# A Fourier-mixing and attention kernel: the sequence DFT as seven products of quarter blocks, and four of five chunks of the output projection moved into the loop

## The chip, the core and the metric

The kernel runs on one core of a Trainium2 chip. A core has a matrix engine (TensorE, PE in the profile; its weight loads are shown apart as PEld), a vector engine (VectorE, DVE), an engine for activation functions (ScalarE, ACT), a general engine (GpSimd, POOL) and one that issues the kernel's DMAs (SyncE, SP; its queue is SPq). They run side by side and wait for each other on semaphores. Data lies in DRAM, in SBUF (128 partitions) and in PSUM, the eight banks that matmuls write. The metric is the device time of one execution in microseconds (us); less is better.

## What is computed

Inputs are x (2048 x 640), the DFT matrices of the sequence (2048 x 2048, real and imaginary) and of the hidden dimension (640 x 640, real and imaginary), the weights of an attention with 32 query heads of width 20 and one shared key/value head, and a gate vector. All is float32.

```python
# A: Fourier mixing                       # B: attention, S=2048, D=640, H=32, Dh=20
a = x @ dft_hid_re.T                      q = (x @ wq) split into 32 heads
b = x @ dft_hid_im.T                      k, v = x @ wk, x @ wv          # shared by all heads
A = dft_seq_re @ a - dft_seq_im @ b       o = softmax(q k^T / sqrt(20)) v
                                          B = concat(o) @ wo
g = sigmoid(sum(x * gate_w, -1))
out = g * A + (1 - g) * B
```

## The kernel before

Float32 products are made from three matmuls: each operand is split into a high part (rounded) and a low part (the rest), and high x high, high x low and low x high are summed in PSUM. The split of one operand is a cast and a subtraction.

A **place** is one pair of matmuls of 64 rows by 320 columns on the two halves of the array (`halves.put` queues a pair, `halves.run` emits one of its two matmuls, written y0 and y1 below). All of part A is done in places: first 64 groups of 15 places make a and b (tile names `ab`, 960 places), then 64 groups of 48 places make the sequence DFT (tile name `y`, 3072 places). A group fills two PSUM banks (F0, F1); when its last matmul is done ACT copies both banks to SBUF (`y_evict`, entries E0 and E1), POOL adds the two halves, and the next group may use the banks.

The rest of the kernel is the attention. `a_unit` makes scores for the row maximum (PE matmul `a`, DVE `mx`), `b_unit` makes them again transposed and takes the exponential (PE `b`, ACT `pt`), `av_step` multiplies by v (PE `av`, V in the plans). The order on PE is written out by hand: 256 rounds `(p, qh, kk)`, head pair by half of the queries by pair of key blocks, each following a list (`AB15`, `Y16`, `Y12`, `N12`) that says in which order the a, b, y, E and V entries go. There are 48 rounds of AB15 with 15 places, 144 of Y16 with 16 places, 54 of Y12 and 10 of N12 with 12 places; N12 has no `a` left to do. A round ends with E0 E1 V V, and the V of a round belongs to the b of the round before. The entries of a round call the generator `f_stream` for as many places as the round has, and with them the loads and splits that the generator issues between its places.

In the DFT stage before, one block of 128 rows by 1024 of the DFT matrix is loaded (`load_c`, 512 KB), split by POOL (`split_c`: `ch` L465, `cl` L466) and used twice, for the two halves of the columns (48 places); the transformed x, split, lies in SBUF (`ab`).

After the last round, the output projection stands alone: `o_group` is called 32 times (16 token blocks, 2 column halves) and makes 5 chunks x 3 = 15 matmuls of 128 rows by 320 columns each, then DVE scales and adds part A (`oy` L558), and SP writes 128 x 320 numbers of the output. The attention output `oT_d` and the broadcast reciprocal of the softmax sums `rx_d` come through DRAM (`load_o`, `mult_o`, `split_o`). `finish_half` ends a half of a head pair: ACT copies the sums and outputs out of PSUM (`ob`), SP writes them to `sum_d` and `oT_d` and reads the sums back reshaped (`sm`); `finish_sums` or, for the last head pair, `finish_last` takes the reciprocal on DVE (`rc`), writes it (`rec_d`) and broadcasts it to 20 rows (`rx_d`). The last half of the last pair is finished after the first `o_group`, and its data are needed by the 17th.

The order on PE, ACT, DVE and POOL is the order in the code. The order on SP is chosen by the scheduler when the program is built and is then fixed, so a DMA that waits holds back the DMAs behind it. `later(n, f, ...)` calls f after n ticks, and a round has four ticks.

Of the kernel before, what the change touches and what calls it, by code (L numbers as in the profile page):

```python
# [17 lines left out]
P = 128  # L18
# [15 lines left out]
def kernel(  # L34
# [30 lines left out]
    class Rot:  # L65
# [11 lines left out]
    ab_d = {  # L77
        (j, e): dram.tile([P, 4 * HALF], F32, name=f"ab_d{j}{e}") for j in range(SJ) for e in range(2)
# [6 lines left out]
    y0_d = dram.tile([S, D], F32, name="y0_d")  # L85
# [204 lines left out]
    PHASES = ((1, 0), (0, 0), (1, 1), (0, 1))  # L290
    XSEQ = [SJ * half + j for half, e in PHASES for j in range(SJ)]
# [165 lines left out]
    def load_c(sh, tb, i):  # L457
        raw = raw_tile([P, SJ, P], "craw")
        move(raw, (cre, cim)[i][tb, sh])
        return raw  # L460

    def split_c(raw):
        n = free_c.pop(0)
        h, l = [c_slot(2 * n + z, [P, SJ, P], F32R, "ch cl".split()[z]) for z in range(2)]
        nc.gpsimd.tensor_copy(h, raw)  # L465
        nc.gpsimd.tensor_tensor(l, raw, h.bitcast(F32), op=ALU.subtract)  # L466
        return h, l, n

    first_c = {}
# [4 lines left out]
    yp = []  # L474

    TW = 2 * P
    wos, oraw, ospl, yrow = {}, {}, {}, {}

    def spare(k, name):
        if k % 4 < 2:  # L480
            return yp[0].tile([P, D], F32, tag=f"spare{k % 4}", name=name, bufs=1)
        return cpool.tile([P, D], F32, tag=f"raw{k % 4 - 2}", name=name)

    wo_raw = {}

    def load_wo(c):
        wo_raw[c] = spare(c % 2, "woraw")
        move(wo_raw[c], wo[c * P : (c + 1) * P])

    def split_wo(c):  # L490
        raw = wo_raw.pop(c)
        if c < 3:
            if c == 0:
                wos["at"] = [t[:, : 3 * HALF] for t in qbuf[:3]]
                wos["at"].append(c_slot(2 * free_c[0], [P, 3 * HALF], F32R, "wo"))
            at = [wos["at"][k // 3][:, k % 3 * HALF : (k % 3 + 1) * HALF] for k in range(4 * c, 4 * c + 4)]
        else:
            t = abp.tile([P, 4, HALF], F32R, tag=f"ab{c - 3}0", name=f"wo{c}")
            at = [t[:, k] for k in range(4)]
        for e in range(2):  # L500
            h, l, r = at[2 * e], at[2 * e + 1], raw[:, e * HALF : (e + 1) * HALF]
            nc.vector.tensor_copy(h, r)
            nc.vector.tensor_tensor(l, r, h.bitcast(F32), op=ALU.subtract)
            wos[c, e] = (h, l)

    oT_v = oT_d.rearrange("(c p) t -> p c t", p=P)
    rx_v = rx_d.rearrange("(c p) t -> p c t", p=P)
    NO = S // TW

    def load_o(n):  # L510

        if n < NO:
            oraw[n] = []
            for k, v in enumerate((oT_v, rx_v)):
                if (n % 2, k) == (1, 1):
                    t = yp[0].tile([P, KC, TW], F32, name="oraw", bufs=1)
                else:
                    t = abp.tile([P, KC, TW], F32, tag=f"ab{5 + 2 * (n % 2) + k}0", name="oraw")
                move(t, v[:, :, n * TW : (n + 1) * TW])
                oraw[n].append(t)  # L520

    def mult_o(n):
        if n < NO:
# [25 lines left out]
    def o_group(tb, e):  # L549
        n, k = divmod(tb, 2)  # L550
        es, tk = slice(e * HALF, (e + 1) * HALF), slice(k * P, (k + 1) * P)
        rows = slice(tb * P, (tb + 1) * P)
        ps = orot(f"o_{tb}_{e}")[:, :HALF]
        h, l = ospl[n]
        for c in range(KC):
            mm3(ps, h[:, c, tk], l[:, c, tk], *wos[c, e], KC, c)
        oy = yp[0].tile([P, HALF], F32, tag=("yt", "yu")[e], name="oy")
        nc.vector.scalar_tensor_tensor(  # L558
            oy, ps, omg[:, tb : tb + 1], yrow[tb][:, es], op0=ALU.mult, op1=ALU.add
        )  # L560
        move(out[rows, es], oy)
# [33 lines left out]
    def ab_sum(grp):  # L595
# [5 lines left out]
        if stage["loop"]:  # L601
            ab_low()
# [102 lines left out]
    def f_stream():  # L705
# [293 lines left out]
```

## Time and profile before

| | |
|---|---|
| median of 3 runs | 1797.76 us (1797.14 to 1797.78) |
| profiled execution, its own time | 1797.24 us |
| its span, first to last instruction | 1795.5 us |
| PE busy | 1782.3 us, 99% of the span |
| DVE, ACT, POOL busy | 1390.7, 1231.5, 551.9 us |
| DMA traffic | 156.44 MB, mean 87 GB/s |

The profile is of one execution. Its own time is 1.74 us more than its span, and 0.52 us less than the median. "Busy" of PE is modelled, since matmuls overlap: the durations of single matmuls are longer than the distance at which they start. Idle time of an engine that nothing waits for costs nothing.

### The profile page before, as it was taken

What the parts mean: (1) busy time and instruction counts of PE and PEld (TensorE: products, weight loads), DVE (VectorE), ACT (ScalarE), POOL (GpSimd) and SP (SyncE); (2) the same over time, 40 slices, a digit from 0 to 9 for tenths busy, and PEclk for the clock granted to TensorE, in tenths of its full rate; (3) what the DMA queues carried; (4) which work ended last, traced back from release to release, by engine and by line L of the source; (5) the groups of instructions that cost most, each with busy time, mean ns of one, the idle gap of its engine ahead of it and who ended that gap; (6) DMA issues with size and microseconds to landing.
All of it is one profiled execution on the core that took longest, in us unless ns stands there. A gap on an engine that the chain in (4) does not pass through costs nothing.

```text
span 1795.5 us, 42902 instructions
## 1 busy us (share of the span) xinstructions
PE 1782.3 (99%) x17112; PEld 1286.0 (72%) x17112; DVE 1390.7 (77%) x2319; ACT 1231.5 (69%) x2421; POOL 551.9 (31%) x492
## 2 busy tenths in 40 slices
PE   8999999999999999999999999999999999999999
PEld 6797677767777777777777777777776666666689
DVE  4498888888888888888888888888888888888334
ACT  3347878887777767777767777776777777777830
POOL 3056575555222221212212123222321221122131
PEclk9999999999999999999999999999999999999999
DMA  7652123211211221111121552222121211111376
GB/s 245 196 184 93 50 87 113 91 51 51 89 48 47 66 64 56 52 56 59 50 65 40 175 178 72 68 63 63 57 66 51 60 48 59 56 52 33 93 226 213
DMA packets 105956, 156.44 MB, mean 87 GB/s; under 512 B 25108, under 2 KB 74772, under 8 KB 105156
## 3 DMA queue, kind: packets, MB, share of 16 engines
q1 hardware_dynamic: 105756, 153.70, 27.2%
q8 instruction: 134, 2.20, 0.5%
q14 instruction: 66, 0.54, 0.1%
HBM read 109.16 MB, written 48.76 MB: 88 GB/s over the span
## 4 chain that ended last, share of the span: by engine, by line
PE 97%; DMA 1%; SPq 1%; DVE 1%; issue 0%; ACT 0%; DVEq 0%; ACTq 0%
PE av L781 26%; PE y L576 23%; PE b L769 19%; PE a L226 15%; PE ab L576 7%; PE o L114 1%; PE o L115 1%; PE o L116 1%; PE q L114 1%; PE q L116 1%; PE q L115 1%; SPq L106 1%; DMA ql_d<-ql 0%; DMA xr<-in_xT_dram 0%; DMA wraw<-in_wq_dram 0%; DVE xl L110 0%
## 5 line engine op out<-in xcount | busy, mean ns | idle before, releaser
L233 DVE TENSOR_REDUCE mx<-a 128x1 f32<-128x512 f32 x2048 | 1278.4, 684 | 269.6 <-PE a L226 228.4
L777 ACT ACTIVATE pt<-b 128x512 f32<-128x512 f32 x2048 | 1074.9, 604 | 365.6 <-PE a L226 284.7
L769 PE MATMUL b<-qs,ks 62*128 62x512 f32 x2048 | 772.8, 415 | 1.7 <-DVE mx L233 1.3
L226 PE MATMUL a<-ks,qs 60*128 60x512 f32 x2048 | 721.1, 410 | 0.2
L576 PE MATMUL y<-ab,ch 64*128 64x320 f32 x4096 | 718.8, 306 | 0.0
L576 PEld LDWEIGHTS y<-ab,ch 64*128 64x128 f32 x4096 | 550.0, 185 | 10.1
L769 PEld LDWEIGHTS b<-qs,ks 62*128 62x128 f32 x2048 | 350.5, 185 | 224.7 <-DVE mx L233 169.4
L576 PE MATMUL y<-ab,cl 64*128 64x320 f32 x2048 | 509.1, 306 | 0.0
L781 PE MATMUL av<-pt,vsb 128*32 128x512 f32 x4096 | 492.5, 598 | 0.0
L226 PEld LDWEIGHTS a<-ks,qs 60*128 60x128 f32 x2048 | 351.4, 185 | 9.9 <-ACT pt L777 1.2
L576 PEld LDWEIGHTS y<-ab,cl 64*128 64x128 f32 x2048 | 320.1, 185 | 6.6
L586 POOL TENSOR_TENSOR yt<-yt,yu 128x320 f32<-128x320 f32 x64 | 55.4, 866 | 696.5 <-ACT yu L581 696.5
L781 PEld LDWEIGHTS av<-pt,vsb 128*32 128x32 f32 x4096 | 106.8, 109 | 223.7 <-issue 214.8
L466 POOL TENSOR_TENSOR cl<-craw,ch 128x1024 fp32r<-128x1024 f32 x64 | 152.8, 2387 | 5.1
L465 POOL CAST ch<-craw 128x1024 fp32r<-128x1024 f32 x64 | 66.6, 1041 | 266.0 <-PE y L576 257.4
L598 POOL TENSOR_TENSOR abt<-abt,abu 128x320 f32<-128x320 f32 x64 | 55.8, 872 | 140.1 <-ACT abu L631 140.1
L576 PE MATMUL ab<-wbh,xh 64*128 64x320 f32 x256 | 58.6, 306 | 0.0
L576 PE MATMUL ab<-wbh,xl 64*128 64x320 f32 x256 | 58.4, 305 | 0.0
L614 POOL TENSOR_TENSOR ab<-abt,ab 128x320 fp32r<-128x320 f32 x64 | 56.2, 878 | 3.9
L576 PE MATMUL ab<-w1l,xh 64*128 64x320 f32 x192 | 50.5, 307 | 0.0
L576 PE MATMUL ab<-w0l,xh 64*128 64x320 f32 x192 | 49.9, 306 | 0.0
L576 PE MATMUL ab<-w0h,xh 64*128 64x320 f32 x192 | 48.3, 308 | 0.0
(103 smaller groups left out, 1427.2 us busy)
## 6 DMA issues: line engine op xcount, KB each, us to landing
craw<-in_cre_dram SPq DMA_DIRECT2D x32, 512.0 KB
craw<-in_cim_dram SPq DMA_DIRECT2D x32, 512.0 KB
xraw<-in_xT_dram SPq DMA_DIRECT2D x32, 320.0 KB
qs<-qh_d SPq DMA_DIRECT2D x128, 80.0 KB
ab_d<-ab SPq DMA_DIRECT2D x16, 640.0 KB
y_d<-yt SPq DMA_DIRECT2D x64, 160.0 KB
ab<-ab_d SPq DMA_DIRECT2D x16, 640.0 KB
xr<-in_xT_dram SPq DMA_DIRECT2D x20, 256.0 KB
```

The source lines that it names most:

```text
L114: nc.tensor.matmul(ps, wh, xh, start=(i == 0), stop=False)
L226: nc.tensor.matmul(ps, qs[v][b : b + 60, qb * P : (qb + 1) * P], ks[b : b + 60, c * ROW : (c + 1) * ROW], start=True, stop=True,)
L233: nc.vector.tensor_reduce(mx[v][:, hh, qb, c : c + 1], ps, axis=AX.X, op=ALU.max)
L465: nc.gpsimd.tensor_copy(h, raw)
L466: nc.gpsimd.tensor_tensor(l, raw, h.bitcast(F32), op=ALU.subtract)
L576: nc.tensor.matmul(ps, w, x, start=start, stop=stop)
L586: nc.gpsimd.tensor_tensor(yt, yt, yu, op=ALU.add)
L598: nc.gpsimd.tensor_tensor(t0, t0, t1, op=ALU.add)
L614: nc.gpsimd.tensor_tensor(lo, t0, hi.bitcast(F32), op=ALU.subtract)
L769: nc.tensor.matmul(ps, ks[b : b + 62, kc * P : (kc + 1) * P], qs[2 * p + qc // 2][b : b + 62, (qc % 2) * ROW : (qc % 2 + 1) * ROW], start= ...
L777: nc.scalar.activation(t, ps, AF.Exp, scale=SCALE)
L781: nc.tensor.matmul(ps[32 * g : 32 * g + 32, :], vsb[:, kc, :], t, start=first, stop=last)
```

## The change

The DFT matrix and the transformed x are cut into quarter blocks, and the 2 x 2 block product is done with seven block products (Strassen's scheme in Winograd's form) where eight were done before. In the code the four A blocks are the upper and the lower 1024 rows of the real and of the imaginary matrix (`a_src`), each 2048 wide. One product has 16 loaded blocks of 128 x 1024 and 8 groups of 48 places, so the seven have 2688 places. The 384 places that are left of 3072 take chunks 0 to 3 of the output projection (32 groups `oo` of 12 places), in the last 32 rounds. The plans of the rounds and their order are as before.

- Every block of a product is loaded, combined from two blocks where the scheme wants a sum (`PRODUCTS`: 64 of 112 blocks, one more POOL operation and one more load each), split, and used once. Two sums are stored to DRAM (`s_d`) and read again.
- The transformed x goes to DRAM unsplit (`b_d`); POOL makes four differences of its blocks during the first product (`sum_t`, to `t_d`), and the operand of products 3 to 7 is loaded and split one product ahead (`load_b`, `split_b`).
- What a product adds to the result is combined on POOL (`y_out`), with partial results that go through DRAM (`part_d`). The gate is applied later, in `o_out`.
- The weights `wo` and the attention output are split on POOL inside the loop, and `o_out` adds the gated part A to the scaled chunks 0 to 3 and leaves the sum in SBUF (`acc`).
- After the loop, `o_group` makes 3 matmuls for chunk 4 instead of 15 for all five, and DVE adds to `acc`. The last 16 of the 32 groups wait for the last half of the last head pair; its reciprocal is now broadcast straight to SBUF (`load_rec`), and product and split are four pieces on DVE (`split_last`).
- `finish_sums` comes 12 ticks after `finish_half` instead of 24, and `finish_half` issues its four sums before its four outputs.

```diff
+    PRODUCTS = (
+        ("p1", (a_src(0, 0),), None, None, None),
+        ("p2", (a_src(1, 0),), None, None, None),
+        ("p5", (a_src(0, 1), a_src(1, 1)), ALU.add, 1, t_d[1]),
+        ("p6", (s_src(1), a_src(0, 0)), ALU.subtract, 2, t_d[2]),
+        ("p7", (a_src(0, 0), a_src(0, 1)), ALU.subtract, None, t_d[3]),
+        ("p3", (a_src(1, 0), s_src(2)), ALU.subtract, None, b_d[1, 1]),
+        ("p4", (a_src(1, 1),), None, None, t_d[4]),
+    )
+    def split_c(g):
+        if g < NP:
+            n, k = divmod(g, NT)
+            raw = c_raw.pop(g)
+            _, _, how, save, _ = PRODUCTS[n]
+            if how:
+                nc.gpsimd.tensor_tensor(raw[0], raw[0], raw[1], op=how)
+            if save:
+                later(3, move, s_d[save][k // 2, k % 2].rearrange("p (j t) -> p j t", j=SJ), raw[0])
...
+            nc.gpsimd.tensor_copy(h, raw[0])
+            nc.gpsimd.tensor_tensor(l, raw[0], h.bitcast(F32), op=ALU.subtract)
...
+    def y_out(name, r, m, parts):
...
+        t = parts[0]
+        add(t, m, ALU.subtract if name == "p4" else ALU.add)
+        if name == "p6":
+            add(parts[1], t)
+            keep("u2", t)
+            keep("u4", parts[1])
+        elif name == "p7":
+            add(parts[1], t)
+            keep("u3", t)
+            done(1, 1, parts[1])
...
+    def o_out(tb, e, m, y0):
...
+        nc.gpsimd.tensor_scalar(y0, y0, gate[:, tb : tb + 1], None, op0=ALU.mult)
+        nc.gpsimd.tensor_tensor(acc[tb][:, e], m, y0, op=ALU.add)
...
+    def load_rec(qh):
+        ts = slice(qh * QT, (qh + 1) * QT)
+        for hh in range(2):
+            b = P - (2 - hh) * DH
+            move(last_o[qh][1][b : b + DH], rec_d[2 * LAST + hh : 2 * LAST + hh + 1, ts].to_broadcast([DH, QT]))
+
+    def split_last(qh, k, n):
...
+        nc.vector.tensor_tensor(o[:, cs], o[:, cs], r[:, cs], op=ALU.mult)
+        nc.vector.tensor_copy(h[:, cs], o[:, cs])
+        nc.vector.tensor_tensor(l[:, cs], o[:, cs], h[:, cs].bitcast(F32), op=ALU.subtract)
...
     def o_group(tb, e):
...
-        for c in range(KC):
-            mm3(ps, h[:, c, tk], l[:, c, tk], *wos[c, e], KC, c)
...
+        mm3(ps, h[:, tk], l[:, tk], *wos[OC, e], 1, 0)
+        t = acc[tb][:, e]
+        nc.vector.scalar_tensor_tensor(t, ps, omg[:, tb : tb + 1], t, op0=ALU.mult, op1=ALU.add)
...
+        for g in range(NP):
...
+            sum_t(g - 1)
+            split_c(g + 1)
+            load_c(g + 2)
+            split_b(g + NT)
+            load_b(g + NT + 1)
...
+        for tb in range(NT):
+            for e in range(2):
+                if e == 0:
+                    split_o(tb + 1)
+                else:
+                    load_o(tb + 2)
...
-            later(24, chores.append, (finish_sums, p, sm))
+            later(12, chores.append, (finish_sums, p, sm))
...
-    for i in range(2 * NT):
+    for i in range(NT):
         tb, e = divmod(i, 2)
         o_group(tb, e)
-        tick()
-        if i == 0:
+        if i == 1:
             for st in old:
                 av_step(*st)
             finish_half(*old[-1][:2])
...
+            load_last(1)
+        elif i >= NT - 4:
+            tick()
+    load_rec(1)
+    for i in range(NT):
+        tb, e = divmod(i, 2)
+        if i % 4 == 0:
+            split_last(1, i // 4, 4)
+        o_group(SJ + tb, e)
```

The first place that the change rewrites is POOL's work between two groups of the DFT. Before, in the second half of the stage, one group of 48 places has this on POOL: `yt` and `yu` are the two halves, `y0` the partial result read back, and the block of the DFT matrix is split once.

```order
L466 TENSOR_TENSOR cl_19242<-craw_19142,ch_19241 128x1024
L586 TENSOR_TENSOR yt_19415<-yt_19415,yu_19416 128x320
L590 TENSOR_TENSOR yt_19415<-yt_19415,y0_19140 128x320
L465 CAST ch_19557<-craw_19447 128x1024
L466 TENSOR_TENSOR cl_19558<-craw_19447,ch_19557 128x1024
```

In the changed kernel one group of the product p6 has this on POOL (`craw` is combined in place, `tb` is the operand of the next product, `part` holds partial results):

```order
L722 TENSOR_TENSOR yt_18051<-yt_18051,yu_18052 128x320
L557 TENSOR_TENSOR part_17747<-part_17747,yt_18051 128x320
L557 TENSOR_TENSOR part_17749<-part_17749,part_17747 128x320
L498 TENSOR_TENSOR craw_17866<-craw_17866,craw_17868 128x1024
L503 CAST ch_18081<-craw_17866 128x1024
L504 TENSOR_TENSOR cl_18082<-craw_17866,ch_18081 128x1024
L521 CAST tb_18089<-braw_17873 128x320
L522 TENSOR_TENSOR tb_18089<-braw_17873,tb_18089 128x320
L498 TENSOR_TENSOR craw_18085<-craw_18085,craw_18087 128x1024
L503 CAST ch_18211<-craw_18085 128x1024
L504 TENSOR_TENSOR cl_18212<-craw_18085,ch_18211 128x1024
L521 CAST tb_18219<-braw_18092 128x320
```

A group that had four POOL operations now has thirteen (the subtraction that ends the second split of `tb` follows the last row), and the three additions of the old group stand ahead of the first block of the new one.

The second place is the end of the program on SP. Before, the last finish of a head pair stands between output writes, and rows of `o_group` that don't need it follow:

```order
L106 DMA sm<-sum_d 64x16
L106 DMA yrow<-y_d 128x640
L106 DMA out_dram<-oy 128x320 x2
L106 DMA yrow<-y_d 128x640
L106 DMA out_dram<-oy 128x320
L106 DMA rec_d<-rc 64x16 x2
L106 DMA out_dram<-oy 128x320
L106 DMA yrow<-y_d 128x640
L106 DMA rx_d<-rec_d 20x1024 x2
L106 DMA out_dram<-oy 128x320
L106 DMA oraw<-oT_d 128x5x256
L106 DMA oraw<-rx_d 128x5x256
```

In the changed kernel:

```order
L110 DMA out_dram<-acc 128x320 x2
L110 DMA sum_d<-ob 1x512 x4
L110 DMA oT_d<-ob 20x512 x4
L110 DMA sm<-sum_d 64x16 x2
L110 DMA out_dram<-acc 128x320 x2
L110 DMA oraw<-oT_d 128x1024
L110 DMA out_dram<-acc 128x320 x12
L110 DMA rec_d<-rc 64x16 x2
L110 DMA oraw<-rec_d 20x1024 x2
L110 DMA out_dram<-acc 128x320 x16
```

Twelve output writes now stand on the queue between the reading of the attention output and the writing of the reciprocal, and the last sixteen come behind the broadcast.

The third place is the end of the program on DVE, at the same point. Before, `oy` of the groups and splits of later blocks surround the reciprocal:

```order
L558 SCALAR_TENSOR_TENSOR oy<-o_1_28311,omg,yrow 128x320
L558 SCALAR_TENSOR_TENSOR oy<-o_0_28332,omg,yrow 128x320
L824 RECIPROCAL rc<-sm 128x16
L558 SCALAR_TENSOR_TENSOR oy<-o_1_28357,omg,yrow 128x320
L558 SCALAR_TENSOR_TENSOR oy<-o_0_28379,omg,yrow 128x320
```

In the changed kernel the reciprocal comes behind all of the first sixteen groups, and each piece of `split_last` is followed by the four groups that use it:

```order
L664 SCALAR_TENSOR_TENSOR acc<-o_1_29980,omg,acc 128x320
L915 RECIPROCAL rc<-sm 128x16
L651 TENSOR_TENSOR oraw<-oraw 128x256
L652 CAST osp<-oraw 128x256
L653 TENSOR_TENSOR osp<-oraw,osp 128x256
L664 SCALAR_TENSOR_TENSOR acc<-o_0_29997,omg,acc 128x320
L664 SCALAR_TENSOR_TENSOR acc<-o_1_30003,omg,acc 128x320
L664 SCALAR_TENSOR_TENSOR acc<-o_0_30009,omg,acc 128x320
L664 SCALAR_TENSOR_TENSOR acc<-o_1_30015,omg,acc 128x320
L651 TENSOR_TENSOR oraw<-oraw 128x256
```

From the reciprocal on, nothing on DVE is independent of the last head pair.

## Rows read from the trace of the kernel before

**Rows 1.** The page: busy time of the engines, share of the span, instructions.

```profile
PE 1782.3 (99%) x17112; PEld 1286.0 (72%) x17112; DVE 1390.7 (77%) x2319; ACT 1231.5 (69%) x2421; POOL 551.9 (31%) x492
```

**Rows 2.** The page: chain of work that ended last, by line.

```profile
PE av L781 26%; PE y L576 23%; PE b L769 19%; PE a L226 15%; PE ab L576 7%; PE o L114 1%; PE o L115 1%; PE o L116 1%; PE q L114 1%; PE q L116 1%; PE q L115 1%; SPq L106 1%; DMA ql_d<-ql 0%; DMA xr<-in_xT_dram 0%; DMA wraw<-in_wq_dram 0%; DVE xl L110 0%
```

**Rows 3.** The chain in order of time: start, length, what; V entries, first `o`.

```profile
1003.49 1.87 PE av L781 x16
...
1041.15 1.85 PE av L781 x16
...
1719.52 0.35 PE o L114
```

**Rows 4.** Timeline of DVE and ACT, end of the program: start, length, [idle before].

```profile
1792.21 0.55 DVE L558 SCALAR_TENSOR_TENSOR oy<-o,omg,yrow 128x320 f32<-128x320 f32 x1 [1.65 <-PE o L116]
...
1723.86 0.60 ACT L792 ACTIVATE ob<-av 128x512 f32<-128x512 f32 x1 [3.78 <-PE av L781]
```

**Rows 5.** Groups by line: count, busy, mean ns of one, idle before.

```profile
L466 POOL TENSOR_TENSOR cl<-craw,ch 128x1024 fp32r<-128x1024 f32 x64 | 152.8, 2387 | 5.1
...
L465 POOL CAST ch<-craw 128x1024 fp32r<-128x1024 f32 x64 | 66.6, 1041 | 266.0 <-PE y L576 257.4 <-PE a L226 8.6
...
L586 POOL TENSOR_TENSOR yt<-yt,yu 128x320 f32<-128x320 f32 x64 | 55.4, 866 | 696.5 <-ACT yu L581 696.5
...
L611 POOL CAST ab<-abt 128x320 fp32r<-128x320 f32 x49 | 22.2, 452 | 3.0
...
L503 DVE TENSOR_TENSOR qs<-woraw,qs 128x320 fp32r<-128x320 f32 x4 | 2.0, 492 | 0.2
```

**Rows 6.** Timeline around the end of a group in Y16.

```profile
1004.77 0.86 POOL L586 TENSOR_TENSOR yt<-yt,yu 128x320 f32<-128x320 f32 x1 [5.54 <-ACT yu L581]
...
1012.14 0.31 PE L576 MATMUL y<-ab,ch 64*128 64x320 f32 x2
```

**Rows 7.** Timeline of SP: rows of the maximum to the next half's queries.

```profile
1034.06 2.80 SPq L106 DMA_DIRECT2D qs<-m_d  x4
```

**Rows 8.** Timeline of ACT: exponentials of a Y12 round; an eviction and two N12 rounds.

```profile
1654.49 4.34 ACT L777 ACTIVATE pt<-b 128x512 f32<-128x512 f32 x8 [2.01 <-PE a L226]
...
1700.09 0.60 ACT L581 ACTIVATE yt<-y,gate 128x320 f32<-128x320 f32 x1
...
1701.00 4.03 ACT L777 ACTIVATE pt<-b 128x512 f32<-128x512 f32 x8
...
1705.75 4.03 ACT L777 ACTIVATE pt<-b 128x512 f32<-128x512 f32 x8 [0.72 <-PE b L769]
```

**Rows 9.** Timeline of SP after the loop: start, time on the queue, what.

```profile
1726.33 0.25 SPq L106 DMA_DIRECT2D sum_d<-ob  x1
...
1728.23 0.49 SPq L106 DMA_DIRECT2D sm<-sum_d  x1
...
1733.81 1.11 SPq L106 DMA_DIRECT2D rec_d<-rc  x2
...
1736.48 1.57 SPq L106 DMA_DIRECT2D rx_d<-rec_d  x2
...
1742.46 0.38 SPq L106 DMA_DIRECT2D oraw<-rx_d  x1
...
1772.08 0.86 SPq L106 DMA_DIRECT2D out_dram<-oy  x2
```

**Rows 10.** Timeline of PE, its first matmuls: start, length, [idle before].

```profile
5.37 0.80 PE L114 MATMUL kv<-xh,kvgh 128*128 128x512 f32 x1 [5.37 <-ACT kvgh L109]
...
9.80 0.63 PE L115 MATMUL q<-xl,wqh 128*128 128x512 f32 x1
10.23 0.63 PE L116 MATMUL q<-xh,wql 128*128 128x512 f32 x1
```

**Rows 11.** Windows: busy of PE, PEld, DVE, ACT, POOL; granted clock, DMA share, GB/s.

```profile
0.00:5.00 5.00, 0.00 (x0) 0.00 (x0) 0.33 (x1) 2.19 (x4) 4.18 (x12) 1.00 0.52 140
...
1748.00:1752.00 4.00, 4.00 (x30) 4.00 (x29) 1.33 (x2) 0.00 (x0) 2.60 (x1) 1.00 1.06 391
```

More of the change, by code (lines that the diff above doesn't have):

```diff
@@ L287, in a_half @@
                 do_chores()
-    PHASES = ((1, 0), (0, 0), (1, 1), (0, 1))
-    XSEQ = [SJ * half + j for half, e in PHASES for j in range(SJ)]
+    XSEQ = [t for e in range(2) for t in range(NT)]
     x_raw, x_now = {}, {}
@@ L455, with a_src @@
     free_c = [0, 1, 2]
[L457 to L469, printed above, removed]
-    ab = {}
+    def a_src(i, th):
+        return lambda r, sh: (cre, cim)[i][SJ * th + r, sh]
@@ new lines, with load_t, sum_t @@
+    t_raw = {}
+    def load_t(k):
+        if k < NT:
+            t_raw[k] = []
+            for z, (i, e) in enumerate(((0, 0), (0, 1), (1, 1), (1, 0))):
+                t = yp[0].tile([P, HALF], F32, tag=f"part{z}", name="braw")
+                move(t, b_d[i, e][k])
+                t_raw[k].append(t)
+    def sum_t(k):
+        if k in t_raw:
+            b11, b12, b22, b21 = t_raw.pop(k)
+            sub = ALU.subtract
+            nc.gpsimd.tensor_tensor(b11, b12, b11, op=sub)
+            nc.gpsimd.tensor_tensor(b12, b22, b12, op=sub)
+            nc.gpsimd.tensor_tensor(b22, b22, b11, op=sub)
+            nc.gpsimd.tensor_tensor(b21, b22, b21, op=sub)
+            for z, t in ((1, b11), (3, b12), (2, b22), (4, b21)):
+                later(3, move, t_d[z][k], t)
@@ L472, with part @@
     pp = ctx.enter_context(tc.tile_pool(name="pp", bufs=16))
     op = ctx.enter_context(tc.tile_pool(name="op", bufs=2))
[L474 to L484, printed above, removed]
+    def part(k, src):
+        t = yp[0].tile([P, HALF], F32, tag=f"part{k}", name="part")
+        move(t, src)
+        return t
@@ L486, in load_wo, with q_tile @@
+    wos, osp = {}, {}
+    oq = {}
+    def q_tile(k, shape, dt, name):
+        return abp.tile(shape, dt, tag=f"ab1{k}", name=name)
     def load_wo(c):
-        wo_raw[c] = spare(c % 2, "woraw")
-        move(wo_raw[c], wo[c * P : (c + 1) * P])
+        if c < KC:
+            oq["wo"] = q_tile(10 + c % 2, [P, D], F32, "woraw")
+            move(oq["wo"], wo[c * P : (c + 1) * P])
     def split_wo(c):
[L491 to L499, printed above, removed]
@@ L558, in o_group @@
[L558 to L561, printed above, removed]
+        h, l = last_hl[qh]
+        mm3(ps, h[:, tk], l[:, tk], *wos[OC, e], 1, 0)
+        t = acc[tb][:, e]
+        nc.vector.scalar_tensor_tensor(t, ps, omg[:, tb : tb + 1], t, op0=ALU.mult, op1=ALU.add)
+        move(out[tb * P : (tb + 1) * P, e * HALF : (e + 1) * HALF], t)
     class Halves:
```

364 lines of the change are left out of this document (187 added, 177 removed).

## The prediction

> **What bounds the kernel now.** I read the busy times first: PE is at work for 1782.3 of 1795.5 us [rows 1]. The chain of waits agrees: it runs through PE's av, y, b and a, and everything that isn't PE has about 2% [rows 2]. So only PE's own work, or a new wait of PE, can move the time. The chain in order of time then divides the span. Six rounds of Y16 take from 1003.49 to 1041.15 us, 6.28 us each, and the loop ends at 1719.52 us, where the first `o` starts [rows 3]. A round of N12 takes 4.75 us, from the first exponential of one to that of the next (1701.00 to 1705.75) [rows 8]. The end of the program is 75.98 us long: 32 groups of 15 matmuls, each group 2.20 us (0.55 us of DVE and 1.65 us in which DVE waits for PE), so 0.147 us a matmul, then the last `oy` and 2.74 us from its end (1792.76) to the end of the span, for the last output [rows 4]. PE doesn't wait there: 480 x 0.147 = 70.4 us, 3.7 us of av and these last 3 us come to its length.
>
> **The loop.** The rounds and their places are the same: 960 + 2688 + 384 is 960 + 3072. PE has the same matmuls of the same shapes in the same order between its entries, so the loop keeps its length unless something new is late for it. Three things could be.
>
> First POOL. A product's group has one block more to split than before, and most blocks are first combined from two. Prices: subtraction of 128 x 1024 2.39 us, cast 1.04, addition of 128 x 320 0.87, cast of 128 x 320 0.45 [rows 5]. The combination is of the subtraction's shape, so I take 2.39. The fullest groups are those of p6 and p7, 16 of them: three additions (2.6), two blocks (2 x 5.82) and twice cast and subtraction of an operand (2 x 1.33), 16.9 us; with about 0.08 us from one operation to the next, 17.7 us. A group lasts three rounds, 18.8 us. POOL fits, with 1 us to spare. The order within the group matters too. Count from the V that follows the group's last matmul (1003.49): POOL's first addition starts at +1.28, since ACT evicts first [rows 6]; the additions end at +3.9, the combination at +6.4, the cast at +7.5 and the low part at +10.0. PE wants this block in the middle of the next round, whose places run from 1012.14 [rows 6] to the V two rounds after the first, at 1016.05, so at about +10.6, and the low part two places later. It is in time by some 0.6 to 1 us. In p1 four subtractions (3.5 us) stand in the place of the combination and two additions: +9.3. Cost taken: 0. From the other side, each us by which the low part is later costs 16 us.
>
> Second ACT. It evicts 88 groups in the loop instead of 64, and in the last 32 rounds one group in every round. In N12 ACT has 4.03 us of exponentials and then 0.72 us of idle time; an eviction took 0.91 us from its start to the next exponential (1700.09 to 1701.00) [rows 8]. Done in each round, that makes 4.94 us of work for a round of 4.75, 0.19 us too much, ten times: +1.9 us. In Y12 ACT stands idle for 2.01 us between the exponentials of two rounds [rows 8], enough for the 0.91; nothing there.
>
> Third SP and the DMAs. In p6 a group moves four blocks in, two out, and about 1 MB of small tiles, some 4 MB in 18.8 us, or 215 GB/s beside the mean of 87 that flows today. The DMA engines moved 391 GB/s when fully busy [rows 11], so they keep up. The block of a group is asked for a group's half ahead (9 us), and two of 512 KB take 2.7 us at that rate. `finish_sums` after 12 ticks is three rounds after its loads, 19 us, and the sums need one DMA there and one back; nothing.
>
> **The end of the program.** 384 of 480 matmuls are gone, 56.3 us of PE. But before, 30 groups hid the chain of the last head pair (`ob`, sums out, sums back, reciprocal out, broadcast). Now it has 14 short groups, so I follow the chain itself, in us after the end of the loop. The two groups ahead of it take 1.1, av 1.85, and `ob` is done at 3.6 (it started 0.1 after av and takes 0.60 [rows 4]). SP issues four sums and four outputs, to 6.1; the sums come back asked for at 7.1 at the latest, since a small DMA lands 1.90 us after its issue (1726.33 to 1728.23 [rows 9]). Then SP has two output writes, a load, and twelve output writes ahead of the reciprocal's, at 0.43 us each (0.86 for two [rows 9]): 7.1 + 15 x 0.44 = 13.7. DVE is earlier: 14 `oy` of 0.55 end at about 11, and the reciprocal, which stands behind them, at 11.3. The two writes of the reciprocal take 1.11 us [rows 9] and land by 16.7; the two broadcasts are issued from 16.1 to 17.6. How long a broadcast to 20 partitions takes, the trace doesn't show. Bounds: 1.90 us as for the sums, or 5.98 us from the first issue, as for the broadcast to DRAM (1736.48, awaited until 1742.46 [rows 9]), which ran beside a load of 640 KB. I take the data at 20, nearer the small one, with 19.3 to 22.1 as bounds.
>
> From there four blocks follow each other, because on DVE each piece of `split_last` stands behind the `oy` of the block before. One operation of 128 x 320 took 0.49 us [rows 5]; for 256 columns I estimate 0.4 for each of the two tensor operations and 0.3 for the cast, 1.15 with gaps. PE answers with the first group 0.74 later, three more at 0.44 each, against which `oy` runs at about 0.5; with the last `oy` a block is 3.95 us. Four are 15.8, and the output 2.74: the end at 38.5.
>
> That is at PE's pace of today. PE, however, has nothing to do from about 10 to 21. The trace shows once what follows: PE had no work for its first 5.37 us, and 4.4 us later its matmuls of 512 columns still started 0.43 us apart (9.80 to 10.23 [rows 10]), which is 1.2 GHz, the lower of its two levels, while 0.147 us for 320 columns is the pace of 2.4 GHz. The column of the granted clock says 1.00 for that stretch too [rows 11], so it can't be asked; the distance of the starts can. At half pace the groups of a block come 0.88 us apart and the block lasts 1.15 + 1.2 + 3 x 0.88 + 0.6 = 5.6 us, 1.65 us more. I take the low pace for most of the four blocks, +5.5 us in all, with 0 and +6.6 as bounds: the end at 44.0.
>
> The Trainium skill says the same of this place (TensorE: Matmul & The Clock Gate, The HAM clock gate): the throttled clock is the default and activity releases it, so that a kernel that feeds PE in bursts between waits pays again for each. By that rule all four blocks would be slow, and the end at 45.1.
>
> **The sum** is made against the profiled execution, 1797.24 us, which is 0.5 us below the median: - 75.98 (the end before) + 44.0 (the end after) + 1.9 (evictions in N12) = 1767.2 us. I predict 1767.
>
> **The rivals.**
>
> *PE keeps its full pace in the end.* For it: rows 10 are of the start of the program, where PE had not worked at all, and no row shows an idle time of 10 us after work. Against it: the rows of the start are the only ones that there are. 1767.2 - 5.5 = 1761.7; with the quicker broadcast 1761.0.
>
> *POOL becomes what PE waits for.* For it: 94% of a group in p6 and p7, and a margin of less than 1 us at one block of each group; the combination in place has no row of its own. Against it: the rows of one shape differ little, and nothing in the group waits for POOL a second time. At 0.5 to 1.2 us late in 16 groups it costs 8 to 19 us: 1775 to 1786.
>
> *The queue holds back the maxima, and the kernel is slower than before.* The rows of the maximum go to DRAM and back into the queries (`qs<-m_d`) before a half's first b. SP issued them from 1034.06 to 1036.86 [rows 7]; they land 1.9 later, at 1038.8, and the b follow the V that ends at 1043.0 [rows 3]: 4.2 us to spare. In the changed kernel the stores of combined blocks and partial results stand ahead of them on SP and wait for POOL, up to 5 us by my count of p6. 22 halves lie in the stage of products. It costs from the point at which SP is over 4.2 us later than now, and the kernel is slower than before from 1.6 us beyond that on each (22 x 1.6 = 35): 1801 or more. Against it: the two delays meet only in some halves, so some 5 us (1772) are likelier than 35.
>
> *The end keeps its gain in full.* If the chain were hidden as before, the time would be 1797.24 - 56.3 + 1.9 = 1742.8. Against it: nothing is left to hide it; SP's order alone puts twelve writes ahead of the reciprocal.
>
> **How the numbers follow.** Slow pace at the end, as summed, 1763 to 1770: 0.48. Full pace, 1757 to 1763: 0.21. POOL late, 1770 to 1787: 0.16. The queue: 0.05 for a few us (within 1768 to 1787), 0.05 for slower than before. Something between 1787 and 1801 that I don't see: 0.03, of it 0.02 within 0.2%. Below 1757: 0.02. The range 1757 to 1785 leaves out about 0.12. A difference of 0.2%, 3.6 us, is about what a measurement of this kernel can tell from no change. Faster by more: 0.93; within it: 0.02; slower: 0.05.
>
> **What would show it.** Rounds of 6.28 us from the first product to p7, no idle time of PE ahead of y for `cl`, rounds of about 4.9 us in the last ten; PE idle for about 10 us after the first 16 groups, waiting for DVE, and DVE for the DMA from `rec_d`; then four bursts of 12 matmuls, their starts 0.28 to 0.29 us apart if the pace is low and 0.15 if it isn't; 44 us from the first `o` to the end. The prediction is wrong if PE waits in p6 and p7 for POOL, if b waits at the boundaries of halves, or if the broadcast takes much longer than 6 us.

## The result, and the profile after

The changed kernel takes 1802.9 us (median of 6 runs, 1800.1 to 1806.8) where the kernel before takes 1797.5 beside it: 1.003 times as long, with 1.0017 to 1.0043 as interval. 1767 was predicted. The profiled execution took 1803.36 us, with a span of 1801.6.

The page, first its busy times, then the chain by line, then the group of the matmuls b (count, then busy and mean, then idle time before and what ended most of it):

```profile
PE 1747.6 (97%) x16728; PEld 1246.0 (69%) x16728; DVE 1372.5 (76%) x2301; ACT 1243.0 (69%) x2470; POOL 1123.1 (62%) x983
...
PE av L869 25%; PE b L857 18%; PE y_p L680 18%; PE a L235 15%; PE ab L680 7%; PE oo L680 3%; DMA m_d<-m 2%; PE q L118 1%; PE q L120 1%; SPq L110 1%; PE q L119 1%; DMA qs<-m_d 1%; DMA wraw<-in_wq_dram 1%; POOL cl L504 1%; DVE acc L664 0%
...
L857 PE MATMUL b<-qs,ks 62*128 62x512 f32 x2048 | 782.0, 419 | 23.5 <-DMA qs<-m_d 20.5
```

PE does 35 us less than before [rows 1], but `m_d<-m` and `qs<-m_d`, the way of the maxima to DRAM and back into the queries, now stand in the chain, and b waits for them. That wait doesn't exist in the kernel before, whose page has this for b:

```profile
L769 PE MATMUL b<-qs,ks 62*128 62x512 f32 x2048 | 772.8, 415 | 1.7 <-DVE mx L233 1.3
```

**The end** is shorter than forecast. DVE's and SP's rows (start, duration; in brackets what ended the idle time before):

```profile
1762.57 1.01 DVE L664 SCALAR_TENSOR_TENSOR acc<-o,omg,acc 128x320 f32<-128x320 f32 x2 [9.11 <-PE o L120]
...
1783.03 0.43 DVE L651 TENSOR_TENSOR oraw<-oraw 128x256 f32<-128x256 f32 x1 [10.73 <-DMA oraw<-rec_d]
...
1787.73 0.41 DVE L651 TENSOR_TENSOR oraw<-oraw 128x256 f32<-128x256 f32 x1
...
1791.35 0.41 DVE L651 TENSOR_TENSOR oraw<-oraw 128x256 f32<-128x256 f32 x1
```

```profile
1770.87 6.49 SPq L110 DMA_DIRECT2D out_dram<-acc  x12
1777.45 1.11 SPq L110 DMA_DIRECT2D rec_d<-rc  x2
1780.19 0.70 SPq L110 DMA_DIRECT2D oraw<-rec_d  x2
```

The first `o` starts at 1761.75, so the end lasts 39.85 us instead of 75.98. The reciprocal stands behind twelve output writes, its data come 21.3 us after the loop, the first of the four blocks takes 4.70 us and the next 3.62.

**The loop** is 42.2 us longer: its end, the first `o`, moved from 1719.52 [rows 3] to 1761.75. Its rounds have kept their lengths (6.28 us in the products, 4.75 in N12). The rest sits at the boundaries of halves. A half has eight rounds; there are 32, counted from 0, and each has its own maximum, which must be back in the queries before the half's first b. From the end of DVE's last operation on the maximum (`m`, 32 in each trace) and the end of SP's last issue of `qs<-m_d` behind it I made this table for the halves 7 to 24, most of the stage of the products:

| half | last `qs<-m_d` issued, us after the maximum: before, after | until the next maximum: longer than before by |
|---|---|---|
| 9 | 4.2, 15.4 | 6.7 |
| 12 | 4.3, 14.2 | 6.0 |
| 15 | 4.2, 16.1 | 7.4 |
| 17 | 4.2, 12.8 | 1.6 |
| 18 | 6.1, 16.7 | 7.9 |
| 21 | 4.2, 15.9 | 6.8 |
| the other twelve | 4.2 to 7.6, 5.5 to 11.5 | under 0.2 each |

The six make 36.3 us. A further 2.5 lie at the first product, where PE waits 1.9 us for POOL's `cl`, 2.3 ahead of the seventh maximum, and 1.2 behind the maximum of half 24; what makes these last two isn't shown. With 36.1 gained at the end that is 1797.24 + 42.2 - 36.1 = 1803.3.

Half 12 shows how it comes. The chain in order of time (start, duration, what), then what SP waited for between the maximum and the last issue (total, times, longest):

```profile
743.83 2.39 POOL cl L504
746.22 0.40 POOL tb L521
...
746.69 0.88 POOL tb L522
...
747.59 0.32 SPq L110
...
748.91 3.51 DMA m_d<-m
...
754.53 2.03 DMA qs<-m_d
...
756.70 0.76 PE b L857
```

```profile
SPq L110 <- POOL tb L522: 4.0, 1, 4.0
SPq L110 <- DMA m_d<-m: 3.0, 1, 3.0
SPq L110 <- POOL craw L498: 2.0, 1, 2.0
```

The maximum is ready at 740.97. Ahead of `m_d<-m` on SP stands, among others, a load of `braw` (747.59) whose buffer POOL must first free. So `m_d` is issued 7.9 us after the maximum instead of 0.03, the first `qs<-m_d` follows it 3.5 us later instead of 1.5, and b starts at 756.70. Before, with the maximum ready at 729.50, SP had this:

```profile
729.52 0.32 SPq L106 DMA_DIRECT2D m_d<-m  x1
730.97 2.78 SPq L106 DMA_DIRECT2D qs<-m_d  x4
```

The windows (PE, PEld, DVE, ACT, POOL busy, granted clock, DMA share, GB/s) show what this does to PE:

```profile
752.00:754.00 2.00, 1.23 (x12) 0.13 (x4) 0.68 (x2) 0.40 (x2) 1.45 (x2) 1.00 0.01 2
754.00:756.00 2.00, 0.69 (x3) 0.29 (x3) 0.24 (x1) 0.22 (x1) 2.00 (x2) 0.97 0.04 6
756.00:758.00 2.00, 1.30 (x8) 1.33 (x10) 1.05 (x2) 0.82 (x2) 1.86 (x3) 0.50 0.57 168
758.00:760.00 2.00, 2.00 (x16) 2.00 (x15) 0.58 (x1) 0.75 (x2) 2.00 (x1) 0.50 1.01 323
760.00:762.00 2.00, 2.00 (x16) 2.00 (x15) 1.40 (x3) 1.54 (x3) 1.92 (x4) 0.50 0.77 270
762.00:764.00 2.00, 2.00 (x18) 1.45 (x19) 1.06 (x2) 1.44 (x3) 1.94 (x2) 0.82 0.75 211
```

PE's two waits for b are 1.99 and 0.79 us long. Then the granted clock is 0.50, the lower level of 1.2 GHz, from 756 to past 762: this half lost 6.0 us, and more than half of that is pace. The clock record of the trace shows the same at five of the six halves, 6.8 us each; half 17, whose waits were 0.56 and 0.58 us, kept 1.00 and lost 1.6 us.

### The profile page after: what moved, and what is told of

The parts are those of the page before. It is cut to its first block, busy times and chain, and to the rows that moved or that the text cites. A ratio compares the mean times of both kernels' runs of the same rounds, so it can differ in the third digit from the quotient of the medians.

```text
span 1801.6 us, 43713 instructions
## 1 busy us (share of the span) xinstructions
PE 1747.6 (97%) x16728; PEld 1246.0 (69%) x16728; DVE 1372.5 (76%) x2301; ACT 1243.0 (69%) x2470; POOL 1123.1 (62%) x983
## 4 chain that ended last, share of the span: by engine, by line
PE 92%; DMA 4%; SPq 1%; POOL 1%; DVE 1%; issue 0%; ACT 0%; DVEq 0%; POOLq 0%; ACTq 0%
PE av L869 25%; PE b L857 18%; PE y_p L680 18%; PE a L235 15%; PE ab L680 7%; PE oo L680 3%; DMA m_d<-m 2%; PE q L118 1%; PE q L120 1%; SPq L110 1%; PE q L119 1%; DMA qs<-m_d 1%; DMA wraw<-in_wq_dram 1%; POOL cl L504 1%; DVE acc L664 0%
## 5 line engine op out<-in xcount | busy, mean ns | idle before, releaser
L680 PE MATMUL y_p<-tb,ch 64*128 64x320 f32 x3584 | 642.9, 310 | 0.0
L680 PEld LDWEIGHTS y_p<-tb,ch 64*128 64x128 f32 x3584 | 488.6, 188 | 8.6 <-POOL ch L503 0.3
L680 PE MATMUL y_p<-tb,cl 64*128 64x320 f32 x1792 | 450.7, 309 | 1.9 <-POOL cl L504 1.9
L680 PEld LDWEIGHTS y_p<-tb,cl 64*128 64x128 f32 x1792 | 280.0, 188 | 7.7 <-POOL cl L504 2.1
L504 POOL TENSOR_TENSOR cl<-craw,ch 128x1024 fp32r<-128x1024 f32 x112 | 267.5, 2388 | 9.0
L498 POOL TENSOR_TENSOR craw<-craw 128x1024 f32<-128x1024 f32 x64 | 153.5, 2398 | 0.0
L503 POOL CAST ch<-craw 128x1024 fp32r<-128x1024 f32 x112 | 116.2, 1038 | 12.8 <-PE a L235 6.5
L680 PE MATMUL oo<-wo,osp 64*128 64x320 f32 x768 | 93.2, 307 | 0.0
L680 PEld LDWEIGHTS oo<-wo,osp 64*128 64x128 f32 x768 | 85.8, 186 | 1.8
L522 POOL TENSOR_TENSOR tb<-braw,tb 128x320 fp32r<-128x320 f32 x80 | 70.1, 876 | 6.4
```

What stands on the lines that cost most here:

```text
L498: nc.gpsimd.tensor_tensor(raw[0], raw[0], raw[1], op=how)
L503: nc.gpsimd.tensor_copy(h, raw[0])
L504: nc.gpsimd.tensor_tensor(l, raw[0], h.bitcast(F32), op=ALU.subtract)
L522: nc.gpsimd.tensor_tensor(t[:, 1], raw, t[:, 0].bitcast(F32), op=ALU.subtract)
L680: nc.tensor.matmul(ps, w, x, start=start, stop=stop)
```

## The experiments

Theory Q (the queue): SP's fixed order holds the maxima back behind DMAs that wait for POOL. Rival T (traffic): 260 MB flow where 156 did, and small transfers are slow. Rivals C and W are in the expectations.

**1. The maxima on ACT's queue.**

```diff
-        move(m_d[v], m3[:, 1:])
...
+            later(1, there)     # nc.scalar.dma_start of m_d
+            later(3, back)      # nc.scalar.dma_start of the four qs
...
```

> The changed kernel, with the five DMAs of each half's maxima (m_d<-m and four qs<-m_d) issued from ACT's queue instead of SP's, one tick and three ticks after the maximum is made; all other DMAs and all work as they are. Theory Q (the queue): in the changed kernel six halves lose 1.7 to 7.9 us, 36.7 in all, because on SP the maxima stand behind DMAs that wait for POOL. Then the six gaps go and the time is about 1803 - 37 = 1766 us, with some us of doubt since ACT issues 160 DMAs more. Theory T (traffic): the maxima come late because 260 MB flow where 156 did, and the small transfers take longer. Then the gaps stay and the time stays above 1790.

1956.9 us, ratio 1.0906 (1.0867 to 1.0946): far off both. No b waits for `qs<-m_d` in any half, but now the exponentials stand behind the issues on ACT, and PE's a behind the exponentials. What ACT and PE waited for (total, times, longest):

```profile
ACT pt L877 <- DMA qs<-m_d: 105.5, 27, 11.7
PE a L235 <- ACT pt L877: 117.3, 30, 12.1
```

The wait of b is gone, and another queue is held up in its place; the last issue itself still comes up to 15.6 us after the maximum where ACT's own work stands ahead of it.

**2. More lead.** `LEAD = 14` instead of 10: the scores for the maximum run one round further ahead of their use.

> The changed kernel with LEAD 14 instead of 10: the scores for the maximum run one round (6.27 us) further ahead of their use, and nothing else is changed. In the changed kernel a half loses time when the last qs<-m_d is issued more than about 12.3 us after the maximum; the latest is at +16.7. With 6.3 us more the bound is 18.6. Theories Q and T: all six gaps go, about 1766 us. Theory C (the gaps at the boundaries of halves have another cause than late maxima, for example POOL or the clock by itself): no gain, 1800 to 1806.

1765.5 us, ratio 0.9825 (0.9810 to 0.9839). C falls. SP is as late as it was (up to 16.5 us after the maximum), but b comes a round later; `qs<-m_d` is no longer among PE's waits:

```profile
PE o L118 <- DVE osp L652: 17.0, 4, 12.8
PE kv L118 <- ACT kvgh L113: 5.7, 1, 5.7
PE b L857 <- DVE mx L242: 1.8, 2, 1.4
PE y_p L680 <- POOL cl L504: 1.6, 1, 1.6
```

**3. Four buffers for `braw`.** `name="braw", bufs=4`.

> The changed kernel with four buffers instead of two for braw, the blocks that are loaded from t_d, so that SP's load of one doesn't wait until POOL has split an earlier one (POOL tb ended 144 us of SP's waits). Theory Q, if this wait is what holds SP: most of 37 us come back, 1766 to 1780. Theory Q, if SP then waits as long for the next store behind it (cl, part, abt): little, 1790 to 1803. Theory T: nothing.

1798.0 us, ratio 1.0002 (0.9991 to 1.0012). It gains some 5 us: half 17 comes under the bound of some 12 us (+10.7) and half 12 loses 2.3 us instead of 6.0, but 9, 12, 15, 18 and 21 still issue `m_d` 7.4 to 10.5 us late, behind the next DMA that waits. Not one buffer holds SP, the order does.

**4. The old kernel with late maxima.**

```diff
-            chores.append((a_final, v))
+            if 8 <= v < 24:
+                later(8, a_final, v)
+            else:
+                chores.append((a_final, v))
```

> The kernel before, where the maxima of 16 halves (8 to 23) are made 8 ticks later, about 10 us, on DVE; nothing of the seven products is in it. The last qs<-m_d is then issued about 14.2 us after the maximum's old place, 1.9 us past the bound of 12.3. Theory Q with the clock: each of the 16 halves loses about 6 us as half 12 of the changed kernel did at +14.2, most of it because PE's granted clock falls to 0.50 after the wait: 1797 + 96 = 1893 us, and the granted clock is near 0.5 for some us behind each boundary. Theory W (only the wait itself costs): 16 x 1.9 = 30 us, 1828. Theory T (it needs the new traffic): under 1815.

1894.3 us, as Q with the clock had it: 96.9 us, 6.05 for each half, without any of the new products. PE's own waits are half of this (total, times, longest):

```profile
PE b L772 <- DMA qs<-m_d: 49.6, 32, 4.6
```

**5. The maxima on ACT, one at a time.** As 1, with `later(3 + k, back, ...)` for the four `qs`.

> As e1, the maxima's five DMAs on ACT's queue, but one at a time: m_d<-m one tick after the maximum, the four qs<-m_d at ticks 3, 4, 5 and 6, so that ACT issues about 0.65 us between two exponentials instead of 2.8 to 4.2 us at once (in e1 PE's a waited 117 us for ACT's pt). The last is issued some 8 to 9 us after the maximum whatever SP does. Theory Q: the six gaps go, 1766 us, and up to 13 us more where ACT's issues don't fit into its idle 2.0 us a round: 1766 to 1780. Theory T: the transfers themselves are slow beside the new traffic, the gaps stay, over 1790.

1844.3 us, ratio 1.0259 (1.0236 to 1.0282), which neither theory had. Again no b waits for `qs<-m_d`, with the same loads and stores, and that speaks against T. The loss is again ACT's. At half 9 it stood at the issue of `m_d`, while the DMAs had a share of 0.95 to 1.00 from 608 to 612 us:

```profile
611.84 0.32 ACTq L259 DMA_DIRECT2D m_d<-m  x1
612.26 1.09 ACT L877 ACTIVATE pt<-b 128x512 f32<-128x512 f32 x2 [6.61 <-DMA braw<-b_d]
```

The 6.61 us include the time in which ACT stood at the issue. The profile names a load of SP's queue, `braw<-b_d`, as what ended them; why the issue would have to wait for it no run here settles.

**6. The old kernel with more lead.** `LEAD = 14` in the kernel before.

> The kernel before with LEAD 14 instead of 10. Theory Q: there the last qs<-m_d was issued at most 9.3 us after the maximum, under the bound of 12.3, so that more lead gives nothing: 1797 us, within 3. If the longer lead saves time by itself (in e2 it could then have done so too): under 1790.

1798.1 us, ratio 1.0008 (0.9999 to 1.0017): lead by itself gives nothing. The 37 us of run 2 are the late maxima's.

**7. The wait filled with work.**

```diff
+        if hh == 0 and kc == 0 and qc % 2 == 0 and 8 <= 2 * p + qc // 2 < 24:
+            for k in range(16):
+                nc.tensor.matmul(
+                    ps,
+                    ks[b : b + 60, :P],
+                    qs[2 * p + qc // 2][b : b + 60, :ROW],
...
```

> As e4 (the kernel before, maxima of 16 halves made 8 ticks late; 1894.3 us), with 16 matmuls of 60 rows by 512 columns more ahead of the first b of each of these halves, written to the bank that this b overwrites: 3.4 us of PE work in the place of the wait, 54 us over the 16 halves. In e4 PE stood idle for 66.8 us ahead of these b, and the loss was 96.6. Theory Q with the clock: the rest of the loss is the half pace after the wait; with PE at work it goes, and each half costs its wait of about 4.2 us or a little more: 1797 + 67 to 80 = 1864 to 1877, with the granted clock near 1.00 behind the boundaries. Theory W' (the rest has nothing to do with PE's idleness): 1894 or more.

1879.3 us: 15 us less than run 4, though PE does 16 matmuls more in each of 16 halves, 0.24 us apart, some 61 us in all. (The 66.8 us of the expectation added PE's and PEld's waits, which overlap; 49.6 is the number.) Of 82.6 us over the kernel before, 61 are this work, 5.9 what is left of the wait for `qs<-m_d`, 4.1 short waits of a for DVE; the rest isn't taken apart. Windows at the same boundary, first of run 4, then of run 7:

```profile
819.00:821.00 2.00, 0.71 (x3) 0.29 (x3) 0.58 (x1) 0.55 (x1) 0.00 (x0) 1.00 0.11 21
821.00:823.00 2.00, 1.74 (x12) 1.77 (x14) 0.71 (x2) 0.64 (x2) 0.00 (x0) 0.54 0.44 135
823.00:825.00 2.00, 2.00 (x18) 1.96 (x17) 1.02 (x2) 0.80 (x2) 0.00 (x0) 0.60 0.04 14
825.00:827.00 2.00, 2.00 (x22) 1.68 (x18) 1.71 (x4) 1.85 (x5) 0.00 (x0) 1.00 0.01 4
```

```profile
816.00:818.00 2.00, 2.00 (x11) 1.57 (x10) 0.00 (x0) 0.00 (x0) 0.00 (x0) 1.00 0.03 5
818.00:820.00 2.00, 2.00 (x18) 1.66 (x17) 0.39 (x1) 0.37 (x1) 0.00 (x0) 1.00 0.52 150
820.00:822.00 2.00, 2.00 (x26) 2.00 (x24) 2.00 (x4) 1.81 (x4) 0.00 (x0) 1.00 0.07 25
```

Here PE was at work, and there is no 0.50. It isn't so at every boundary. By the clock records, the granted clock fell at 15 of 16 boundaries of run 4, for 78.5 us in all, and in run 7 at three, for 10.2 us. At these three the matmuls didn't fill the whole wait: b still waited 1.3 to 1.6 us. The first of them:

```profile
931.00:933.00 2.00, 2.00 (x19) 2.00 (x18) 0.32 (x1) 1.19 (x2) 0.00 (x0) 0.54 0.82 291
933.00:935.00 2.00, 2.00 (x19) 2.00 (x18) 1.44 (x3) 1.31 (x3) 0.00 (x0) 0.60 0.34 88
```

These three halves cost 7.8 to 8.1 us; eleven in which b didn't wait cost 4.2 to 4.3. In run 4 the one half that kept 1.00 lost 2.8 us, the others 4.3 to 8.2. So most of the other half of the price of late maxima is the clock: 78.5 us at half pace are up to 39 of the 47 us that aren't wait.

**8. The end on ACT's queue.** Run 2, with `nc.scalar.dma_start` for the last `rec_d` and `oraw<-rec_d`.

> e2 (the changed kernel with LEAD 14, 1765.5 us), with the two writes of the last reciprocal and its two broadcasts on ACT's queue instead of SP's. In the changed kernel the reciprocal was made at 1772.3 and its write was issued at 1777.45, behind twelve output writes on SP. Theory: the chain of the end is shortened by these 5.1 us: 1760.4. Rival: the sums' way back or the broadcast is what takes the time, whatever the queue: 1764 to 1766.

1764.2 us, ratio 0.9818 (0.9804 to 0.9833): what the rival had, and not clear of run 2 (1764.3 to 1768.5 there, 1761.5 to 1766.4 here). The mechanism lies between the two. In the profile the end lasts 37.5 us instead of 40.1: the reciprocal is written at once, but its way takes 8.2 us (1735.30 to 1743.52) instead of 5.5, now that the output writes flow beside it:

```profile
1743.52 0.43 DVE L655 TENSOR_TENSOR oraw<-oraw 128x256 f32<-128x256 f32 x1 [8.26 <-DMA oraw<-rec_d]
```

```profile
1735.30 1.15 ACTq L113 DMA_DIRECT2D rec_d<-rc  x2
1739.24 1.24 ACTq L113 DMA_DIRECT2D oraw<-rec_d  x2
```

**9. The old kernel with more traffic.** Two `later(2 * k, move, extra[...], cre[kk, k])` a round, rounds 48 to 191.

> The kernel before, with two copies of 512 KB a round from the DFT matrix to DRAM tiles that nothing reads, in rounds 48 to 191: 151 MB more, where the change added 104 MB; some 160 GB/s more in the stage of the products. None of these DMAs waits for POOL. Theory T: the small transfers of the maxima then take so long that b waits for them, as in the changed kernel: 20 us or more over 1797. Theory Q: they land 1 to 3 us later, which is within the 12.3 us (the old kernel issues the last at most 7.7 us after the maximum in this stage): 1797 to 1800.

1941.6 us, ratio 1.0811 (1.0796 to 1.0826). But the dose was wrong: nothing tied these copies to their round, SP's fixed order had them all in the first 830 us, and the page shows up to 323 GB/s there. At half 9, whose maximum is ready at 702.41, SP's rows:

```profile
715.89 0.33 SPq L106 DMA_DIRECT2D m_d<-m  x1
716.27 1.77 SPq L106 DMA_DIRECT2D extra<-in_cre_dram  x2
725.89 2.81 SPq L106 DMA_DIRECT2D qs<-m_d  x4
```

Both theories are at work. `m_d` is issued 13.5 us after the maximum, since SP waits for copies of its own (12.8 us from 702 to 729), and from its issue to that of the first `qs<-m_d` it then takes 10.0 us, 1.5 before. So T's mechanism exists, but this run doesn't price it alone.

**10. More work for POOL.** Run 2 with `nc.gpsimd.tensor_copy(h, raw[0])` done twice in p6 and p7.

> e2 (the changed kernel with LEAD 14, 1765.5 us), with the cast of every block of p6 and p7 done twice on POOL: 2.1 us more in each of 16 groups, where POOL stood idle 1.45 us of 18.8 in e2. By the prediction's count POOL has about 1 us to spare; then POOL becomes what PE waits for in these 16 groups, 0.7 to 0.9 us each, 11 to 15 us in all after the first delay is used up: 1775 to 1781, more if PE's waits bring the low clock with them. Rival: POOL's lateness is taken up by slack that the count doesn't see: 1765.

1783.1 us, ratio 0.9923 (0.9909 to 0.9936), a little over the expected range: 17.6 us over run 2. PE waits 15 times for POOL, where it did once in run 2; these waits are 10.9 us, and what makes the rest isn't shown:

```profile
PE y_p L682 <- POOL cl L506: 10.9, 15, 1.9
```

**11. The whole end.** Run 8 with the first 16 output writes on ACT behind the broadcasts, and the reciprocal two groups earlier.

> e8, with the output writes of the first 16 groups issued from ACT's queue too, behind the last broadcasts, and the last reciprocal two groups earlier on DVE. In e8 the write of the reciprocal and the broadcast took 8.2 us from the first issue to the data, against 5.5 us in e2, where the twelve output writes had been issued before. If these writes, flowing beside them, made the difference, the data come 2.7 us earlier than in e8, and up to 1 us more for the reciprocal: 1760 to 1761. If the queue of ACT itself is slower than SP's: as e8, 1763 to 1764.

1761.0 us, ratio 0.9804 (0.9791 to 0.9818), 36 us under the kernel before and the lowest median here, though its runs (1759.8 to 1765.3) overlap with those of run 8. The end lasts 34.2 us. With no output writes beside it the way takes 5.7 us again, from 1734.61 to 1740.35:

```profile
1740.35 0.42 DVE L655 TENSOR_TENSOR oraw<-oraw 128x256 f32<-128x256 f32 x1 [4.93 <-DMA oraw<-rec_d]
```

**12. The traffic of 9, held to its round.**

```diff
+    def more(k):
+        nc.gpsimd.memset(xsrc[:, :1], 0.0)
+        for z in range(2):
+            move(extra[(2 * k + z) % 8], xsrc)
...
+        if 48 <= ROUNDS.index(rnd) < 192:
+            later(2, more, kk)
```

> As e9, but the additional traffic is held to its round: in each of the rounds 48 to 191 POOL writes one column of a 416 KB tile and SP then stores the tile twice to DRAM, 120 MB in all, 133 GB/s more over the 900 us of the products (in e9 all of it ran in the first 830 us, at up to 323 GB/s, and m_d took 8 to 10 us to land). The total of some 200 GB/s is that of the changed kernel there (160 to 221 GB/s at the boundaries that lose). Theory T: b waits for the maxima at many boundaries, 20 us or more over 1797. Theory Q: m_d lands 1 to 2 us later than its 1.4, within the bound: 1797 to 1801.

1802.2 us, ratio 1.0024 (1.0014 to 1.0034): 4.4 us for 159 to 281 GB/s in the page's slices of the products, and PE waits 2.2 us for `qs<-m_d`. Two halves (18 and 19) are together 3.4 us longer than before; at 18 it took 8.2 us from `m_d` to the first `qs<-m_d`:

```profile
1030.23 0.32 SPq L106 DMA_DIRECT2D m_d<-m  x1
1038.45 3.75 SPq L106 DMA_DIRECT2D qs<-m_d  x4
```

The mean hides where the traffic flowed. From the maximum to the last `qs<-m_d` it was 10 to 14 GB/s in the halves 9, 12, 15 and 21, four of the six that lose in the changed kernel, so for these run 12 tests nothing. In the other halves from 7 to 23, at 108 to 247 GB/s, that way took 2.2 to 3.5 us, but for 18 and 19 (8.2 and 5.0).

The rows of the changed kernel weigh the two. In the six halves `m_d` was issued 5.9 to 10.9 us late, and its way was 1.2 to 2.9 us longer in five of them. Without the lateness the last issues would lie at 5.4 to 7.1 us, where nothing is lost; without the longer way at 10.2 to 16.7, and only half 17 clearly under the bound. Run 1 agrees: in six halves with no hold-up on ACT (8, 11, 12, 14, 20 and 23) the last issue came at 5.2 to 6.7 us, beside the other DMAs of the changed kernel. So the queue is the larger part and the traffic adds to it; no run prices the two apart.

## Why the prediction was wrong, point by point

**The step that failed** is the third of "The loop": "Third SP and the DMAs ... nothing". It asked whether bandwidth suffices and whether a block comes in time, and both held in the main. It didn't ask what stands behind a DMA that waits. The rival "The queue holds back the maxima" did, and it is what happened, 36.3 us at the boundaries of six halves; its chance was 0.10 with the slower kernel at 0.05. Its sizes failed three times:
- The delay: "up to 5 us by my count of p6". `m_d` was issued 5.9 to 10.9 us late in the six halves, since several DMAs that wait for POOL stand one after another, and from its issue to that of the first `qs<-m_d` it took 2.6 to 4.3 us instead of 1.5 (3.3 in half 18).
- The spare time: 4.2 us, so the last issue up to +10.3. Nothing was lost up to +11.5; this erred on the other side.
- The price: only the wait was counted. Run 4 shows that the wait is about half, and runs 4 and 7 that most of the rest is PE at 1.2 GHz behind it. So "some 5 us (1772) are likelier than 35" was right that only some of the 22 halves pay, six, and had the price wrong: 6 to 8 us in five of them, 1.6 in half 17.

**POOL** at cost 0 was right for the full groups; the 1.9 us for `cl` at the first product weren't foreseen. In run 2 it stood idle 1.45 us of a group in p6 where 1.1 were counted, and run 10 shows that no 2.1 us more would have fitted.

**ACT in N12**: 0 instead of 1.9. The rounds stayed at 4.75 us: from the first exponential to the first eviction it is 3.83 us (1743.28 to 1747.11), because the last exponential overlaps what follows; 4.03, its full length, was the wrong term.

**The end**: 39.85 instead of 44.0. The data came at 21.3 (20 taken, 22.1 the bound): the reciprocal was written at 15.7 instead of 13.7, mostly since the twelve output writes took 0.54 us each on SP and not 0.44, and its way was then shorter than taken. Blocks at full pace took 3.62 us instead of 3.95, and the low pace was mis-sized: of the 5.5 us only about 1.1 came, in the first block. After 12.75 us without work PE's granted clock is 0.50 in the first block and 1.00 in the second (windows as above):

```profile
1784.00:1786.00 2.00, 2.00 (x8) 2.00 (x9) 0.88 (x3) 0.00 (x0) 0.00 (x0) 0.50 0.00 0
1786.00:1788.00 2.00, 1.15 (x6) 0.89 (x4) 1.75 (x4) 0.00 (x0) 0.00 (x0) 0.82 0.45 164
1788.00:1792.00 4.00, 2.19 (x12) 1.76 (x12) 3.32 (x9) 0.00 (x0) 0.00 (x0) 1.00 0.47 171
```

The Trainium skill (TensorE: Matmul & The Clock Gate, The HAM clock gate) has a kernel that feeds PE in bursts pay again for each. In its example the waits are longer than the three pauses between the blocks here (1.37 to 1.43 us), which cost nothing; the 45.1 us, all four blocks slow, took the rule too far. The boundaries of halves are where it fits: the granted clock fell at five of the six that lose in the changed kernel, and at 15 of 16 in run 4.

**The sum with the maxima in time**: 1797.24 - 75.98 + 39.85 + 6.0 (2.3, 2.5 and 1.2 in the loop) = 1767.1. Run 2 measured 1765.5. That this is nearly the forecast's number is luck: the end and N12 were taken 6.0 us too long, and 6.0 us in the loop weren't foreseen.

Two slips in the working move nothing: the check of the old end's length counts 3.7 us of av where one pair of V, 1.85 us, stands behind the first `o`, and thirteen operations of POOL with 0.08 us between them make 17.9 us, not 17.7.

## What to carry to other kernels

When a change adds DMAs that wait for a slow engine, list what is issued behind them in the same queue and who needs it when: a transfer with a few us to spare is lost first, though bandwidth is ample. Give the slack where it is free (here one round more of lead) before moving transfers to a queue whose engine is itself on the path. Count a new wait of PE at about twice its length when the row shows the granted clock at 0.50 behind it, and give an experiment on traffic a dependence that holds it in its place, or it runs where the queue likes.

## What the runs showed of the hardware

- After waits of PE of 1.99 and 0.79 us the granted clock stood at 0.50 for 6.8 us (half 12). With late maxima it fell at 15 of 16 boundaries (run 4); with the wait filled with matmuls at three, each with 1.3 to 1.6 us of wait left (run 7).
- The way of `m_d` to the first `qs<-m_d`, 1.5 us in most halves of the products in the old kernel, took 2.6 to 4.3 us at 160 to 222 GB/s in the six halves that lose, and 9.3 to 11.3 us in the first eleven halves of run 9.
- A DMA that ACT issues can hold the exponentials behind it for 6.6 us (run 5); the profile names a load of SP's queue as what ended it, and why isn't shown. The Trainium skill (DMA: Bandwidth & Descriptors, Issuing engines are not separate DMA queues) says that issuing from several engines saves only the time to issue. Runs 8 and 11 agree in part: moving the reciprocal's two writes and two broadcasts to ACT took away their place behind twelve others, 5.1 us in the changed kernel, but the data came only some 2.5 us sooner behind the reciprocal until those writes were out of the way too.
